# Four turned spectra instead of three, later products, and a last half chunk rebuilt by matmuls in the first convolution of an S4 and attention kernel

## The chip, the cores and the metric

The kernel runs on one core of a Trainium2 chip. The metric is the device time of one execution in microseconds (us). Before the change the median is 611.42 us over 3 runs (610.12 to 612.61). Engines are named as in the profile: PE is TensorE, PEld its weight loads, DVE is VectorE, ACT is ScalarE, POOL is GpSimd, SP is SyncE, which here issues the DMAs.

Times inside an execution ("229.3") are microseconds from the start of the profiled span.

## The reference, cut to what matters

```python
x = A_u                                                    # (1, 2048, 512), bf16
x = x + _A_ref(_layernorm(x), A_re, ..., log_dt, Dskip)    # the first conv: all of the change
x = x + _B_ref(_layernorm(x), wqkv, wo)                    # sliding local attention
x = x + _A_ref(_layernorm(x), ...)                         # same conv kernel again
x = x + _B_ref(_layernorm(x), wqkv, wo)

def _A_ref(u, ...):                                        # cut
    P = exp(dt * A * l)                                    # D=512 channels, N=128 states, L=2048 positions
    K = einsum("dn,dnl,dn->dl", Cc, P, dB).real            # the convolution kernel of each channel
    y = irfft(rfft(pad(u)) * rfft(pad(K)))[:L]             # FFT convolution over 2L
    return y + u * Dskip
```

Only the first conv builds `K`; the second reuses its spectra from DRAM.

## The kernel before

The first conv goes through eight half chunks of 64 channels, called stages 0 to 7 here (`hc` in the code). In each stage VectorE builds a table of powers (`seed`, `base`, then three `high` operations, then the `y_products` by `MPA` and `MPB`), and PE contracts the table to `K` (`contract`). Between them, chunk by chunk (128 channels), runs the FFT convolution. Its steps for a chunk are:

- a spectrum in two DFT factors: `first` (PE), copy to `Z` (ACT), `turn` (a transposing DMA of 256 KB into `zt`), `second` (PE), copy to `xc` or `Kt` (ACT);
- four products `pa`, `pb` of the signal's and the kernel's spectrum (DVE);
- four inverses (PE) and copies to `VT` (ACT), then `final` (PE) and copies to `X` (ACT).

The products of chunks 0, 1 and 2 come in stages 3, 5 and 7. Those of chunk 3 come in the tail, after the last table.

```python
class Conv:
    def __init__(...):
        self.xbar, self.ahead = True, 3
        self.w = tile_pool(name="f_w", bufs=self.ahead)     # slots of zt; KTq uses the same slots (tag "zt")

    def spectrum(self, rhs_j, n, dsts, drow=None):          # cut
        def turn(i):
            zt = self.w.tile([128, 4, 2, 128], BF, name="zt", tag="zt")
            nc.sync.dma_start(zt..., Z[:, i * 4:i * 4 + 4]..., transpose=True)
        def second(i):
            ...                                             # 4 matmuls from zt, copy by ScalarE to dsts[i]
            if i + self.ahead < cs:
                turn(i + self.ahead)                        # the fourth turn only after the first second
```

```python
# the order of stages 3 and 5: t are the table's steps (t[2] = high, t[3] = MPA, t[4] = MPB), ks the kernel's
# spectrum, p the products, v the inverses
play(t[:2], ks[5:6], [store], ks[6:7], p[:2], ks[7:9], p[2:3], v[:1], p[3:], v[1:3], t[2:3], v[3:], [fin],
     ks[9:], t[3:], [lambda: residual(dc)])

def contract(self, T, Y2, hc, half=None):                   # cut
    if half != 1:
        self.KTq = self.kq.tile([128, 1024], BF, name="KTq", tag="zt")
    nc.scalar.copy(KTq..., psk...)
    return lambda: nc.sync.dma_start(self.kscr[hc]..., KTq...)   # to DRAM, fetched back in another order

def spectrum32(self, KT, drow, dst, ps, Z):                 # half a chunk's spectrum, for the tail (cut)
    def first(jh):
        ...                                                 # half the positions at a time
        (nc.scalar.copy if jh == 0 else nc.vector.tensor_copy)(Z..., ps...)
    def turn():                                             # PE transposes
        ...
        (nc.vector.tensor_copy if r == 0 else nc.scalar.copy)(zt[:, r, :], pt[:, r]...)
    def second():
        ...
        (nc.scalar.copy if r == 0 else nc.vector.tensor_copy)(dst[:, r, :], xp[:])
```

Of the kernel before, what the change touches and what calls it, by code (L numbers as in the profile page):

```python
# [11 lines left out]
ALU = mybir.AluOpType  # L12
AX = mybir.AxisListType
F32 = mybir.dt.float32
BF = mybir.dt.bfloat16
# [4 lines left out]
D = 512  # L20
# [74 lines left out]
def make_consts(nc, const, C):  # L95
    fc = _fft_consts()
    bones_np = np.zeros((128, 4, 32), dtype=np.float32)
    for f in range(128):
        for k in range(4):
            bones_np[f, k, 8 * k + f // 16] = 1.0  # L100
    for name in ("F1", "F1T"):
        C[name + "_h"] = nc.inline_tensor(_bf(fc[name]), name="c_" + name)
    todo = [("ident", _bf(np.eye(128)), BF), ("C2", _bf(fc["C2"]), BF), ("IC", _bf(fc["IC"]), BF),
            ("onesr", _bf(np.ones((1, 128))), BF)]
    for name, arr, dt in todo:
        C[name] = load_const(nc, const, name, arr, dt)
    C["bones_np"] = _bf(bones_np)

# [30 lines left out]
class LnStats:  # L139


    def __init__(self, nc, pool, parts, nm, eps, tag=""):
        self.nc, self.parts, self.eps = nc, parts, eps
        self.st = pool.tile([128, NJ, len(parts), 6], F32, name="ln_st_" + nm, tag="ln_st" + tag)
        self.mv = pool.tile([128, NJ, 2], F32, name="ln_mv_" + nm, tag="ln_mv" + tag)
        self.den = pool.tile([128, NJ], BF, name="ln_den_" + nm, tag="ln_den" + tag)
        self.rstd = pool.tile([128, NJ], F32, name="ln_rstd_" + nm, tag="ln_rstd" + tag)
        self.nb = pool.tile([128, NJ], F32, name="ln_nb_" + nm, tag="ln_nb" + tag)
# [18 lines left out]
class Conv:  # L167


    def __init__(self, nc, tc, es, C, X, psA, psT, zbufs=2, pbufs=2, vbufs=1):  # L170
# [3 lines left out]
        self.xbar, self.ahead = True, 3  # L174
# [62 lines left out]
    def finish(self, dc, xc, Kt):  # L237

        nc, IC = self.nc, self.C["IC"]
        VT = self.one.tile([128, 2, NJ, DCH], BF, name="VT", tag="VT", bufs=self.vbufs)  # L240
        prod = {}

        def product(c):
            prod[c] = self.products(c, xc, Kt)

        def inverse(c):
            pa, pb = prod.pop(c)
            vp = self.pst([128, 2, 32, 2, 8])
            for g in range(4):
                sl = slice(g * 128, (g + 1) * 128)  # L250
                o = vp[:, g // 2, :, g % 2, :]
                nc.tensor.matmul(o, pa[:, 0, sl], IC[:, 0, :], start=True, stop=False)
                nc.tensor.matmul(o, pb[:, 1, sl], IC[:, 1, :], start=False, stop=False)
                nc.tensor.matmul(o, pb[:, 0, sl], IC[:, 2, :], start=False, stop=False)
                nc.tensor.matmul(o, pa[:, 1, sl], IC[:, 2, :], start=False, stop=True)  # L255
            self.vt_evac(c, vp, VT)

        return ([lambda c=c: product(c) for c in range(4)], [lambda c=c: inverse(c) for c in range(4)],
                lambda: self.final(dc, 0, DCH, VT, 8))

    def products(self, c, xc, Kt):
# [5 lines left out]
        return pa, pb  # L267

# [9 lines left out]

    def block(self, c, xc, Kt, VT):

        nc, IC = self.nc, self.C["IC"]
        y = self.w.tile([128, 2, 512], BF, name="y", tag="zt")

        def product():
            pa, pb = self.products(c, xc, Kt)
            nc.vector.tensor_tensor(y[:, 0, :], pa[:, 0, :], pb[:, 1, :], ALU.subtract)
            nc.vector.tensor_tensor(y[:, 1, :], pa[:, 1, :], pb[:, 0, :], ALU.add)

        def inverse():
            vp = self.pst([128, 2, 32, 2, 8])  # L290
            for g in range(4):
                sl = slice(g * 128, (g + 1) * 128)
                o = vp[:, g // 2, :, g % 2, :]
                nc.tensor.matmul(o, y[:, 0, sl], IC[:, 0, :], start=True, stop=False)
                nc.tensor.matmul(o, y[:, 1, sl], IC[:, 2, :], start=False, stop=True)
            self.vt_evac(c, vp, VT, (None, nc.vector if c == 3 else None))
        return [product, inverse]
# [20 lines left out]

    def spectrum32(self, KT, drow, dst, ps, Z):

# [3 lines left out]
        def first(jh):  # L324
            for j in range(jh * 8, jh * 8 + 8):
                for r in range(2):
                    o = ps[:, r, :, j * 8:(j + 1) * 8]
                    dk = j == 0 and r == 0
                    nc.tensor.matmul(o, F1[:, j, r, :], KT[:, :, j, :], start=True, stop=not dk)
                    if dk:  # L330
                        nc.tensor.matmul(o, self.C["onesr"][:], drow, start=False, stop=True)
            sl = slice(jh * 64, jh * 64 + 64)
            (nc.scalar.copy if jh == 0 else nc.vector.tensor_copy)(Z[:, :, :, sl].rearrange("p g r k -> p r g k"),
                                                                   ps[:, :, :, sl])

        def turn():
            pt = self.psT.tile([128, 2, 4, 128], BF, name="pt", tag="psT")
            zt = self.w.tile([128, 2, 512], BF, name="zt", tag="zt")
            for r in range(2):
                for g in range(4):  # L340
                    nc.tensor.transpose(pt[:, r, g, :], Z[:, g, r, :], ident[:])
                (nc.vector.tensor_copy if r == 0 else nc.scalar.copy)(zt[:, r, :],
                                                                      pt[:, r].rearrange("q g k -> q (g k)"))
            box.append(zt)

        def second():
            zt = box.pop()
            for r, (a, b) in ((0, (0, 2)), (1, (1, 0))):
                xp = self.psT.tile([128, 512], F32, name="xpu", tag="psT")
                nc.tensor.matmul(xp[:], C2[:, a, :], zt[:, 0, :], start=True, stop=False)  # L350
                nc.tensor.matmul(xp[:], C2[:, b, :], zt[:, 1, :], start=False, stop=True)
                (nc.scalar.copy if r == 0 else nc.vector.tensor_copy)(dst[:, r, :], xp[:])
        return [lambda: first(0), lambda: first(1), turn, second]
# [16 lines left out]
class Multipliers:  # L370


    def __init__(self, pool):
        self.one = pool.tile([128, 8, 2, HD, 2], BF, name="MU1")
# [227 lines left out]
def kernel_and_first_conv(nc, tc, C, prm, x2d, const, kt_dram, kscr, ln, eps):  # L602
    with ExitStack() as es:
        mt = es.enter_context(tc.tile_pool(name="k_mt", bufs=1))
        M = Multipliers(mt)
        cb = mt.tile([128, 8, HD, 2, 2], BF, name="cb")
        psk = es.enter_context(tc.tile_pool(name="k_psk", bufs=1, space=PSUM))
        T = Tables(nc, tc, es, M, cb, psk, kscr)
        with tc.tile_pool(name="k_prep", bufs=1) as pp, tc.tile_pool(name="k_pst", bufs=2, space=PSUM) as pst:
            raw = load_params(nc, pp, prm)  # L610
# [16 lines left out]
        ln_b = LnStats(nc, const, [(0, 3 * DCH), (3 * DCH, D - 64), (D - 64, D)], "b", eps)  # L627
# [51 lines left out]
        def k_fft(KT, dc, h0=0, h1=2):  # L679
            n = (h1 - h0) * 64  # L680
            drow = skip_row(dc)[:, h0 * 64:h0 * 64 + n]
# [11 lines left out]
        VTs, fetches = [], []  # L693

        def tail(store, ks, p, v, fin, t):
            play(t[:2], ks[5:6], [store])
            KT = k_fetch(3, 0, 1)
            play(ks[6:7], p[:2], ks[7:9], p[2:3], v[:1], p[3:], v[1:2])
            k3 = k_fft(KT, 3, 0, 1)
            Kt, xc = Kts[3], xcs.pop(3)  # L700
            Drow = skip_row(3)
            play(k3[:4], ks[9:], k3[4:5], v[2:3], t[2:3], v[3:], [fin], t[3:4])
            store = contract(7, 0)
            play(k3[5:7], [store, lambda: residual(3)])
            KT = kp.tile([128, 2, 4, NJ, 8], BF, name="KTu", tag="KT")

            def fetch(u):
                return nc.sync.dma_start(KT[:, u].rearrange("p g j d -> p g (j d)"),
                                         kscr[7][:, :, u * 128:u * 128 + 128].rearrange("g p x -> p g x"))
            fetch(0)  # L710
            play(t[4:])
            store = contract(7, 1)
            store()
            fetches.append(fetch(1))
            VT = cv.one.tile([128, 2, NJ, DCH], BF, name="VT", tag="VT", bufs=1)
            VTs.append(VT)
            for c in range(2):
                play(cv.block(c, xc, Kt, VT))
            Z = cv.z.tile([128, 16, 2, 128], BF, name="Z", tag="Z")
            u = [cv.spectrum32(KT[:, n], Drow[:, 64 + n * 32:96 + n * 32], Kt[:, 2 + n],  # L720
                               psk.tile([128, 2, 4, 128], F32, name="psu", tag="psk") if n == 0 else
                               cv.pst([128, 2, 4, 128]), Z[:, n * 4:n * 4 + 4]) for n in range(2)]
            ln_b.gather(X, 0, 0, 6)
            play(u[0][:2])
            cv.final(3, 0, 64, VT, 8)
            ln_b.gather(X, 0, 6, 9)
            play(u[0][2:3])
            ln_b.gather(X, 0, 9, NJ)
            play(u[0][3:4], u[1][:2])
            b = cv.block(2, xc, Kt, VT)  # L730
            play(b[:1], u[1][2:3], b[1:], u[1][3:])
            ln_b.gather(X, 1, 0, NJ)
            play(cv.block(3, xc, Kt, VT))

        with tc.manual_schedule():
            us = u_fft(0)
            play(tables(0), us[:5])
            for hc in range(1, 8):
# [11 lines left out]
                else:  # L750
                    store = contract(hc - 1)
                    p, v, fin = cv.finish(dc - 1, xcs.pop(dc - 1), Kts.pop(dc - 1))
                    if hc == 7:
                        break
                    play(t[:2], ks[5:6], [store], ks[6:7], p[:2], ks[7:9], p[2:3], v[:1], p[3:], v[1:3], t[2:3], v[3:], [fin],
                         ks[9:], t[3:], [lambda: residual(dc)])
            tail(store, ks, p, v, fin, t)
        nc.sync.dma_start(kt_dram[3], Kts[3][:])
        VT = VTs[0]
# [6 lines left out]
        cv.final(3, 64, 128, VT, 4, after)  # L766
# [318 lines left out]
def kernel(  # L1085
# [25 lines left out]
    ln = LnStats(nc, const, [(0, D)], "a", eps)  # L1111
    X, ln_b, marks, last_fetch = kernel_and_first_conv(nc, tc, C, prm, A_u[0], const, kt_dram, kscr, ln, eps)
# [41 lines left out]
```

## Time and profile before

The first conv takes 36 to 264 us of the 607. VectorE is its busiest engine. The page's first part, kernel before (busy us, share of the span, instructions):

```profile
span 607.3 us, 13074 instructions
PE 429.0 (71%) x5646; PEld 285.4 (47%) x5674; DVE 497.4 (82%) x835; ACT 323.5 (53%) x458; POOL 12.6 (2%) x50
```

Busy time in windows, kernel before. The columns are the window, its length, then the busy us and instructions of each engine, the granted TensorE clock, the DMA share and GB/s:

```profile
36.00:62.00 26.00, 2.98 (x16) 1.68 (x16) 25.41 (x43) 26.00 (x43) 0.00 (x0) 1.00 0.00 0
62.00:99.00 37.00, 22.12 (x605) 14.26 (x605) 36.17 (x39) 17.59 (x20) 0.47 (x4) 0.90 0.56 101
229.30:261.10 31.80, 17.60 (x290) 11.56 (x291) 21.46 (x55) 10.91 (x18) 6.06 (x1) 0.75 0.44 135
```

In the first two windows VectorE is busy nearly throughout (25.41 of 26, 36.17 of 37; in the first ScalarE is full as well). From 99 us on, only its waits before the products interrupt it, as the next view shows, so there a saved VectorE wait is saved time. In the third, the tail, nothing is full: VectorE 21.5 of 31.8, PE 17.6, ACT 10.9. That is a chain of hops between engines.

Where VectorE stands still before the tail, its timeline shows. These are the `pa` products of stage 3 (start, busy us, operation, and in brackets the idle time before it and what ended it; the lines between them are left out):

```profile
109.59 0.69 DVE L265 TENSOR_TENSOR pa<-xc,Kt 128x1024 bf16<-128x1024 bf16 x1 [1.71 <-ACT Kt L221]
112.35 0.69 DVE L265 TENSOR_TENSOR pa<-xc,Kt 128x1024 bf16<-128x1024 bf16 x1 [1.47 <-ACT Kt L221]
118.93 0.69 DVE L265 TENSOR_TENSOR pa<-xc,Kt 128x1024 bf16<-128x1024 bf16 x1 [5.29 <-issue]
120.68 0.69 DVE L265 TENSOR_TENSOR pa<-xc,Kt 128x1024 bf16<-128x1024 bf16 x1 [0.45 <-issue]
```

The four brackets add up to 8.9 us. The same sums are 6.5 us in stage 5 and 5.2 us in stage 7: 20.6 us in all. The view of waits, VectorE from 99 to 222 us (total us, times, longest):

```profile
DVE pa L265 <- ACT Kt L221: 14.0, 6, 3.6
DVE pa L265 <- issue: 6.6, 4, 5.3
```

These are the only waits of VectorE in that stretch. SyncE's timeline says why `Kt` is late. In stage 3 the first three turns are issued at 103.03, 105.24 and 106.64, but the fourth only at 111.30, when a slot of `zt` is free; it lands at 114.34. By the order of the code the slot that the first `second` gives back (it ends at 107.59) goes to `KTq`, whose copy starts at 107.63. The fourth turn gets the slot of the next `second`, which ends at 111.27. PE kept to the order of the code meanwhile: the first pair of products ends at 110.89 and both accumulator tiles are copied out by 113.24, but the inverse starts only at 115.30, behind the four matmuls of the fourth `second` (from 114.39), for whose turn PE stood idle 2.25 us.

### The profile page before, as it was taken

The page shows a single profiled execution, that of the slowest core. Times are in us where ns is not written, and L with a number is a line of the kernel's source. Part 1 is how long each engine was busy: PE and PEld are TensorE (multiplying, and loading weights), DVE is VectorE, ACT ScalarE, POOL GpSimd, SP SyncE. Part 2 cuts the span into 40 slices and gives each one's busy share as a digit, 9 for nine tenths or more (in the row PEclk, how much of TensorE's full clock was granted, in tenths as well). Part 3 has the DMA queues.
Part 4 walks back from the last instruction along what each step waited for, and adds up shares of the span by engine and source line. Part 5 has one row for each costly group of instructions (what it writes and reads, how often), then busy time and mean ns, then how long its engine had stood idle before and what let it go on. Part 6 is the DMA issues. An engine that isn't in the chain of part 4 may idle for free.

```text
span 607.3 us, 13074 instructions
## 1 busy us (share of the span) xinstructions
PE 429.0 (71%) x5646; PEld 285.4 (47%) x5674; DVE 497.4 (82%) x835; ACT 323.5 (53%) x458; POOL 12.6 (2%) x50
## 2 busy tenths in 40 slices
PE   1101575665685687479987779978995899858996
PEld 0101343453362465254365566656764434727763
DVE  5999999499699877765977899859999588689950
ACT  4999644454463555236584223467973556722144
POOL 0000000000000003000000000000000000000000
PEclk9999978898897698659998699989998799968999
DMA  9100464635546545400004060000000000040011
GB/s 287 68 1 0 69 108 89 146 50 103 90 105 124 88 123 128 156 0 1 2 2 115 6 257 23 1 1 1 1 2 1 2 0 2 1 121 1 2 70 70
DMA packets 56031, 36.62 MB, mean 60 GB/s; under 512 B 46762, under 2 KB 51754, under 8 KB 54694
## 3 DMA queue, kind: packets, MB, share of 16 engines
q1 hardware_dynamic: 54390, 35.40, 23.2%
q8 instruction: 44, 0.72, 0.5%
q10 hardware_dynamic: 1584, 0.39, 0.3%
q14 instruction: 13, 0.11, 0.1%
HBM read 15.90 MB, written 8.39 MB: 40 GB/s over the span
## 4 chain that ended last, share of the span: by engine, by line
PE 25%; DVE 22%; ACT 7%; issue 6%; POOL 0%; POOLq 0%; ACTq 0%
PE ps_qk L930 8%; DVE prod L1032 6%; PE ps_o L1056 4%; PE ps_v L942 4%; DVE ln_st_b L153 2%; PE Lp L976 2%; PE pt_x L910 2%; PE po L1047 2%; DVE pa L827 2%; DVE pb L828 1%; DVE prod L971 1%; DVE VT L850 1%; DVE zt L809 1%; PE ps_o L1058 1%; ACT oT L1050 1%
## 5 line engine op out<-in xcount | busy, mean ns | idle before, releaser
L1047 PE MATMUL po<-sb_ident,prod 128*128 128x128 bf16 x1024 | 71.5, 230 | 12.6 <-DVE prod L1032 9.1
L1047 PEld LDWEIGHTS <-prod 128*128 128x128 bf16 x1024 | 63.6, 103 | 22.1 <-DVE prod L1032 18.8
L930 PE MATMUL ps_qk<-xnT,wqk 128*128 128x512 bf16 x245 | 64.2, 393 | 4.4 <-ACT xnT L915 2.3
L963 DVE TENSOR_TENSOR prod<-qT,kT 128x2048 bf16<-128x2048 bf16 (+3 forms) x48 | 43.2, 952 | 14.2 <-ACT qT L932 7.2
L195 PEld LDWEIGHTS <-sb_F 128*128 128x128 bf16 x256 | 21.6, 123 | 58.0 <-issue 56.8
L1032 DVE TENSOR_TENSOR prod<-V,L 128x2048 bf16<-128x2048 bf16 (+3 forms) x48 | 43.6, 947 | 6.4 <-PE po L1047 6.4
L1050 ACT CAST oT<-po 128x1024 bf16<-128x1024 f32 x16 | 15.4, 1015 | 56.6 <-PE po L1047 56.6
L195 PE MATMUL psA<-X,sb_F 128*128 128x128 bf16 x128 | 13.3, 255 | 42.4 <-ACT X L624 33.2
L971 DVE TENSOR_TENSOR prod<-qT,kT 128x2048 bf16<-128x2048 bf16 (+3 forms) x40 | 34.9, 902 | 6.9 <-ACT kT L932 4.3
L930 PEld LDWEIGHTS <-wqk 128*128 128x128 bf16 x256 | 23.6, 101 | 32.5 <-issue 12.4
L1056 PE MATMUL ps_o<-wo_t,oT 128*128 128x512 bf16 x121 | 33.5, 380 | 4.7 <-ACT oT L1050 3.9
L1032 DVE TENSOR_TENSOR prod<-Vp,L 128x2048 bf16<-128x2048 bf16 (+3 forms) x40 | 34.9, 896 | 0.0
L198 ACT CAST Z<-psA 128x1024 bf16<-128x1024 f32 (+1 forms) x32 | 29.0, 966 | 9.7 <-PE psA L195 9.7
L976 PE MATMUL Lp<-prod,sb_bones 128*32 128x512 bf16 x256 | 25.4, 416 | 9.6 <-DVE prod L971 4.9
L584 PE MATMUL psk<-Ttab 128*32 128x64 bf16 x1024 | 22.2, 204 | 13.3 <-issue 13.3
L217 PE MATMUL psA<-zt,sb_C 128*128 128x512 bf16 x30 | 12.9, 430 | 25.4 <-DMA zt<-Z 24.7
L942 PE MATMUL ps_v<-wv,xnT 128*128 128x256 bf16 x256 | 28.6, 273 | 1.7 <-ACT V L945 1.7
L594 ACT CAST KTq<-psk 128x1024 bf16<-128x1024 f32 (+1 forms) x9 | 8.3, 918 | 39.5 <-PE psA L220 38.8
L265 DVE TENSOR_TENSOR pa<-xc,Kt 128x1024 bf16<-128x1024 bf16 x16 | 11.0, 690 | 22.0 <-ACT Kt L221 15.4
L566 DVE TENSOR_TENSOR Ttab<-Ttab,MPA 128x2048 bf16<-128x2048 bf16 (+2 forms) x20 | 27.7, 1432 | 0.0
L275 ACT CAST VT<-psA 128x512 bf16<-128x512 f32 x31 | 16.7, 589 | 20.5 <-PE psA L255 9.9
L942 PEld LDWEIGHTS <-xnT 128*128 128x128 bf16 x256 | 25.0, 98 | 5.3 <-issue 2.1
(193 smaller groups left out, 1084.4 us busy)
## 6 DMA issues: line engine op xcount, KB each, us to landing
X<-in_A_u_dram SPq DMA_DIRECT2D x8, 512.0 KB, 5.3
kt_scratch<-Kt SPq DMA_DIRECT2D x4, 1024.0 KB
Kt<-kt_scratch SPq DMA_DIRECT2D x4, 1024.0 KB, 7.9
Vp<-V SPq DMA_DIRECT2D x2, 1568.0 KB
out_dram<-X SPq DMA_DIRECT2D x4, 512.0 KB, 2.6
k_scratch<-KTq SPq DMA_DIRECT2D x7, 256.0 KB, 2.3
KT<-k_scratch SPq DMA_DIRECT2D x7, 256.0 KB, 2.8
sb_F<-c_F SPq DMA_DIRECT2D x1, 1024.0 KB, 7.3
```

The source lines that it names most:

```text
L195: nc.tensor.matmul(o, F1[:, j, r, :], rhs_j(j), start=True, stop=not dk)
L198: nc.scalar.copy(Z[:, 0:n // 8, :, jq * 32:(jq + 1) * 32].rearrange("p g r k -> p r g k"), ps[:, :, 0:n // 8, :])
L566: nc.vector.tensor_tensor(dst, src.to_broadcast([128, q, n, 2 * EYB]), mm.to_broadcast([128, q * n, EYB, 2]), ALU.mult)
L584: nc.tensor.matmul(o.rearrange("e (s i) -> e s i", s=2), xs, T[:, 1:3, h, m // 2, :, t], start=(m == 0), stop=False, skip_group_check=True)
L930: nc.tensor.matmul(ps[:], wqk[:, ct, f0:f0 + 128], xnT[:, ct, s0:s0 + 512], start=(ct == 0), stop=(ct == 3))
L942: nc.tensor.matmul(ps[:, jj].rearrange("p t h d -> p (t h d)"), xnT[:, ct, (j + jj) * 128:(j + jj + 1) * 128], wv[:, ct, a * 256:(a + 1) * ...
L963: nc.vector.tensor_tensor(pr[:, :, (ja - j0) * 128:(ja - j0) * 128 + n], qT[fp][:, :, ja * 128: ja * 128 + n], kT[fp][:, :, (ja - sh) * 12 ...
L971: nc.vector.tensor_tensor(pr[:, :, 0:n], qT[fp][:, :, q0: q0 + n], kT[fp][:, :, k0: k0 + n], ALU.mult)
L976: nc.tensor.matmul(Lp[r0:r0 + 32, w // 4, :], bones[:, w % 4, :], pr[:, f2, hb * 512:(hb + 1) * 512], start=(w % 4 == 0), stop=(w % 4 == 3 ...
L1032: nc.vector.tensor_tensor(p2[:, ja - j0: ja - j0 + n, :].rearrange("p j (t d h) -> p (j t) d h", t=2, d=DH), src.rearrange("p j (t d h) -> ...
L1047: nc.tensor.matmul(po[f2][:, jj, :], p2[:, jj, f2 * 128:(f2 + 1) * 128], ident[:], start=(w == 0 and jj % 4 == 0), stop=(w == W - 1), skip ...
L1056: nc.tensor.matmul(ps[:], oT[:, ft, j * 128:(j + 1) * 128], wo_t[:, ft, :], start=(ft == 0), stop=False)
```

## The change

Its intent:

1. Four turned spectra in flight (`ahead` 3 to 4). To find the room, the layernorm statistics move to other memory.
2. In stages 3 and 5 the `high` operations are issued ahead of the first product and the `MPA` operations between the second and third, so that VectorE has work while it would wait. In stage 7 `high` moves likewise.
3. A new tail. The last half chunk's `K` no longer goes to DRAM and back to be reordered; matmuls with a 0/1 matrix (`spread`) move its rows. The copies of the tail move from VectorE to ScalarE, and statistics fill VectorE meanwhile.

```diff
-        self.xbar, self.ahead = True, 3
+        self.xbar, self.ahead = True, 4
```
```diff
-                    play(t[:2], ks[5:6], [store], ks[6:7], p[:2], ks[7:9], p[2:3], v[:1], p[3:], v[1:3], t[2:3], v[3:], [fin],
-                         ks[9:], t[3:], [lambda: residual(dc)])
+                    play(t[:2], ks[5:6], [store], ks[6:9], t[2:3], p[:2], v[:1], t[3:4], p[2:3], v[1:2], p[3:], v[2:], [fin],
+                         ks[9:], t[4:], [lambda: residual(dc)])
```
```diff
+    spread = np.zeros((128, 4, 132), dtype=np.float32)
+    for p in range(128):
+        spread[p, p // 32, 4 * (p % 32) + 3] = 1.0
...
+            def spread_rows(n):
+                kq = T.KTq[:, n * 512:n * 512 + 512].rearrange("p (c x) -> p c x", c=4)
+                pk = psT.tile([128, 4, NJ, 8], F32, name="pk", tag="psT")
+                for g in range(4):
+                    for c in range(4):
+                        nc.tensor.matmul(pk[:, g].rearrange("p j d -> p (j d)"), spread[:, g, 3 - c:131 - c],
+                                         kq[:, c], start=(g == 0 and c == 0), stop=(c == 3), skip_group_check=True)
+                nc.scalar.copy(KTu[:, n].rearrange("p j g d -> p g j d"), pk[:])
...
-            (nc.scalar.copy if jh == 0 else nc.vector.tensor_copy)(Z[:, :, :, sl].rearrange("p g r k -> p r g k"),
-                                                                   ps[:, :, :, sl])
+            nc.scalar.copy(Z[:].rearrange("p g r k -> p r g k"), ps[:])
...
+            spread_rows(0)
+            contract(7, 1)
+            play(u[0][:1])
+            spread_rows(1)
+            ln_b.gather(X, 0, 0, NJ)
...
+            play(u[0][2:3], k3[5:6], u[1][:1], u[0][3:4], k3[6:7], u[1][2:3], b[:1], [fin], b[2:3], binv[:1], u[1][3:], b[1:2],
+                 binv[2:3], b[3:], binv[1:2], binv[3:])
...
-        cv.final(3, 64, 128, VT, 4, after)
+        cv.final(3, 0, 128, VT, 4, after)
```

## The prediction

> **What bounds it now.** Only the first conv (36 to 264 us of 607) changes. VectorE (DVE) bounds it: the busy-time windows give it 25.4 of 26 us at 36-62, 32.2 of 33 at 62-95, 31.2 of 33 at 167-200. Its idle time is before the `pa` products (DVE timeline): stage 3 1.71 + 1.47 + 5.29 + 0.45 = 8.9 us, stage 5 6.5, stage 7 5.2; the view of waits puts 15.4 us on `Kt` (ACT) and 6.6 on issue, where the two product buffers wait for the inverse. Then the last table ends at 229.3 and the last `VT` copy at 261.1: 31.8 us with DVE busy 21.5, PE 17.6: a chain of hops.
>
> **Mechanism.** The fourth turn (DMA transpose) waits for a free slot: in stage 3 it is issued at 111.30, the third at 106.64, and lands at 114.34. The four seconds precede the inverse in PE's queue, so the inverse waits, then the products. Turns issued together are spaced about 1.3 us, so the fourth should land some 3 us earlier. One is 256 KB; [...] bursts of about 210 GB/s, 1.25 us.
>
> **Stages 3, 5, 7.** The instruction order puts the three `high` operations (3.67 us) ahead of the first product, and in stages 3 and 5 the `MPA` operations (3.4 us) between the second and third. No DVE work is removed. The store of `KTq` no longer queues behind the fourth turn (142.59 in stage 4), so the next `KT` fetch comes about 3 us earlier.
> - Stage 3: all 8.9 us hidden.
> - Stage 5: DVE arrives 9 us earlier, PE's chain only 5 to 6; 2 to 3 us of wait remain: gain 4.
> - Stage 7: likewise, and only `high` moved: gain 2.
>
> Together 15 us at the end of the last table.
>
> **Tail.** Removed: store and fetch of both halves of the last half chunk (2.5 + 5.1 us per trip), and 4.3 us of DVE copies (Z, zt, Kt, VT), now on ACT. Added: 32 selection matmuls [...] and two 0.6 us ACT copies. The 16 statistics (estimated 0.34 us each from the 384- and 64-column ones: 5.4 us) fill DVE while PE rebuilds. Estimated last table to last `VT` copy: 24 to 29 us against 31.8, gain 3 to 8. Later layers only start earlier. The weight load waits for the second selection, still before its use.
>
> **Prediction.** 611.4 - 20 = 591 us, 8 in 10 within 584 to 598. Faster by over 2%: 0.90; within: 0.09; slower: 0.01.
>
> **Right or wrong in the profile.** Four turns at 1.3 us spacing; stage 3 products without `Kt` waits; DVE waits on `pa` down from 22 to 6-9 us; last table operation ending near 214; first `xn` (264.4 before) near 243-245; no `k_scratch` traffic for chunk 7; later stages unchanged in length.
>
> **What would make it wrong.** PE becoming the bound of stages 5 and 7: PE plus its DMA waits is an estimated 40 us per two stages, against 42 of DVE work; more throttling (granted 0.85 there) would bring the waits back. In the tail everything is on ACT and an in-order PE with two accumulator tiles; at the clock of 0.58 seen at 245-265 the chain could be as long as before.

The sum was 15 us at the end of the last table and 3 to 8 us in the tail, together taken as 20: 611.4 - 20 = 591 us. The estimated 40 us of PE can be read from the trace: in the 48.9 us of stages 4 and 5 (132.0 to 180.9) PE was busy for 30.7 us and waited 11.0 us for DMAs, 41.7 us in all, and VectorE was busy for 41.6 us. The "in-order PE" is what stage 3 above shows (the inverse at 115.30 behind the fourth `second` at 114.39). That a clock below the 0.85 of 167 to 200 us would bring the waits back was a guess, which no run tests.

## More of the kernel before

VectorE in the tail (cut to the chain of the first 32 channels):

```profile
234.85 2.85 DVE L153 BATCH_NORM_STATS2 ln_st_b<-X 128x6 f32<-128x384 bf16 x6
239.19 0.69 DVE L333 CAST Z<-psu 128x512 bf16<-128x512 f32 x1 [1.50 <-ACT Z L333]
239.80 1.47 DVE L153 BATCH_NORM_STATS2 ln_st_b<-X 128x6 f32<-128x384 bf16 x3
241.91 0.42 DVE L342 COPY zt<-pt 128x512 bf16<-128x512 bf16 x1 [0.63 <-PE pt L341]
242.25 3.31 DVE L153 BATCH_NORM_STATS2 ln_st_b<-X 128x6 f32<-128x384 bf16 x7
245.47 0.68 DVE L352 CAST Kt<-xpu 128x512 bf16<-128x512 f32 x1
```

The copies of the chain (`Z`, `zt`, `Kt`) stand in VectorE's queue between the layernorm statistics of the next layer. ACT wrote the other half of `zt` by 243.40, but this half of `Kt` follows only at 245.47, behind seven statistics.

## The result and the profile after

The changed kernel takes 588.36 us (median of 4 runs, 585.19 to 590.48) beside 611.27 us (610.12 to 612.61). The ratio is 0.962, with a 95% interval of 0.957 to 0.967. A ratio here is the mean time of one kernel's fast runs over that of the other's of the same rounds, so it is not quite the ratio of the medians.

The page's first part, kernel after, then its windows with the new tail as the third:

```profile
span 586.6 us, 13076 instructions
PE 429.5 (73%) x5670; PEld 281.0 (48%) x5670; DVE 492.5 (84%) x828; ACT 326.5 (56%) x459; POOL 12.6 (2%) x50
```

```profile
36.00:62.00 26.00, 2.98 (x16) 1.67 (x16) 25.41 (x44) 26.00 (x43) 0.00 (x0) 1.00 0.00 0
62.00:99.00 37.00, 22.78 (x617) 14.27 (x617) 36.18 (x39) 19.28 (x21) 0.47 (x4) 0.89 0.56 101
217.10:236.60 19.50, 16.60 (x316) 11.71 (x314) 15.46 (x44) 15.99 (x23) 6.06 (x1) 1.00 0.57 188
```

Up to 99 us VectorE's busy time is the same. The tail is 19.5 us long instead of 31.8, and PE and ACT are now busy in over four fifths of it.

VectorE in stage 3, kernel after (the end of `high`, the `pa` products and `MPA`; the lines between them are left out):

```profile
110.27 1.23 DVE L548 TENSOR_TENSOR Ttab<-Ttab,tx 128x2048 bf16<-128x2048 bf16 x1
111.41 0.68 DVE L270 TENSOR_TENSOR pa<-xc,Kt 128x1024 bf16<-128x1024 bf16 x1
112.61 0.69 DVE L270 TENSOR_TENSOR pa<-xc,Kt 128x1024 bf16<-128x1024 bf16 x1
113.82 3.42 DVE L566 TENSOR_TENSOR Ttab<-Ttab,MPA 128x2048 bf16<-128x2048 bf16 x2
117.16 0.68 DVE L270 TENSOR_TENSOR pa<-xc,Kt 128x1024 bf16<-128x1024 bf16 x1
118.36 0.68 DVE L270 TENSOR_TENSOR pa<-xc,Kt 128x1024 bf16<-128x1024 bf16 x1
```

No bracket is left: `high` and `MPA` stand where the waits were. The four turns are issued at 101.20, 103.36, 104.66 and 106.24, and the fourth lands at 110.28. The view of waits, VectorE from 99 to 222 us, kernel after:

```profile
DVE pa L270 <- ACT Kt L226: 6.2, 3, 2.7
DVE pa L270 <- issue: 2.9, 2, 2.4
```

The 20.6 us are now 9.0 us: none in stage 3, 2.7 us in stage 5, 6.3 us in stage 7.

VectorE in the new tail, kernel after (cut to the statistics and the products before which it waits):

```profile
216.97 5.32 DVE L158 BATCH_NORM_STATS2 ln_st_b<-X 128x6 f32<-128x256 bf16 x16
223.94 0.69 DVE L270 TENSOR_TENSOR pa<-xc,Kt 128x1024 bf16<-128x1024 bf16 x1 [1.65 <-ACT Kt L226]
...
230.36 0.69 DVE L270 TENSOR_TENSOR pa<-xc,Kt 128x1024 bf16<-128x1024 bf16 x1 [2.21 <-ACT X L316]
```

The copies of the chain are on ScalarE now, and the statistics run while VectorE has nothing else to do.

The gain of 20.7 us of span falls into four stretches, read from the traces (the last table operation is the last `Y2tab` product; the last `VT` copy ends the tail; the first attention product is the first `prod<-qT,kT`):

| stretch | before | after | gain |
|---|---|---|---|
| start to end of the last table operation | 229.3 | 217.1 | 12.2 |
| to the end of the last `VT` copy (tail) | 31.8 | 19.5 | 12.3 |
| to the first attention product | 19.6 | 22.6 | -3.0 |
| to the end | 326.6 | 327.5 | -0.9 |

Two gains of 12 us stand against a loss of 3 us at the entry of the attention. The experiments ask which part of the change made each.

### The profile page after: what moved, and what is told of

It is laid out like the page before. It is cut to its first block, busy times and chain, and to the rows that moved or that the text cites. A ratio compares the mean times of both kernels' runs of the same rounds, so it can differ in the third digit from the quotient of the medians.

```text
span 586.6 us, 13076 instructions
## 1 busy us (share of the span) xinstructions
PE 429.5 (73%) x5670; PEld 281.0 (48%) x5670; DVE 492.5 (84%) x828; ACT 326.5 (56%) x459; POOL 12.6 (2%) x50
## 4 chain that ended last, share of the span: by engine, by line
PE 35%; DVE 25%; ACT 20%; issue 9%; DMA 8%; SPq 1%; POOL 0%; ACTq 0%; POOLq 0%; DVEq 0%
PE ps_qk L933 8%; DVE prod L1035 6%; DMA zt<-Z 4%; PE ps_o L1059 4%; PE ps_v L945 4%; ACT Z L203 3%; PE Lp L979 2%; ACT X L625 2%; PE po L1050 2%; PE pt_x L913 2%; DVE ln_st_b L158 2%; PE psA L200 2%; DVE pa L830 2%; DVE pb L831 2%; DVE prod L974 2%
## 5 line engine op out<-in xcount | busy, mean ns | idle before, releaser
L1050 PE MATMUL po<-sb_ident,prod 128*128 128x128 bf16 x1024 | 71.8, 230 | 12.2 <-DVE prod L1035 8.7
L933 PE MATMUL ps_qk<-xnT,wqk 128*128 128x512 bf16 x256 | 65.9, 395 | 4.9 <-ACT xnT L918 2.3
L200 PEld LDWEIGHTS <-sb_F 128*128 128x128 bf16 x256 | 18.9, 112 | 59.4 <-issue 58.6
L200 PE MATMUL psA<-X,sb_F 128*128 128x128 bf16 x128 | 12.2, 238 | 43.4 <-ACT X L625 33.3
L974 DVE TENSOR_TENSOR prod<-qT,kT 128x2048 bf16<-128x2048 bf16 (+3 forms) x40 | 34.9, 900 | 6.9 <-ACT kT L935 4.3
L566 DVE TENSOR_TENSOR Y2tab<-Ttab,MPB 128x6144 bf16<-128x6144 bf16 (+1 forms) x13 | 27.2, 2118 | 0.0
L1062 ACT CAST X<-ps_o 128x512 bf16<-128x512 f32 x32 | 18.2, 586 | 15.2 <-PE ps_o L1061 15.2
L935 ACT CAST kT<-ps_qk 128x512 bf16<-128x512 f32 x32 | 18.8, 590 | 12.5 <-PE ps_qk L933 12.3
```

Of the source, the lines that this page charges most:

```text
L200: nc.tensor.matmul(o, F1[:, j, r, :], rhs_j(j), start=True, stop=not dk)
L566: nc.vector.tensor_tensor(dst, src.to_broadcast([128, q, n, 2 * EYB]), mm.to_broadcast([128, q * n, EYB, 2]), ALU.mult)
L933: nc.tensor.matmul(ps[:], wqk[:, ct, f0:f0 + 128], xnT[:, ct, s0:s0 + 512], start=(ct == 0), stop=(ct == 3))
L974: nc.vector.tensor_tensor(pr[:, :, 0:n], qT[fp][:, :, q0: q0 + n], kT[fp][:, :, k0: k0 + n], ALU.mult)
L1050: nc.tensor.matmul(po[f2][:, jj, :], p2[:, jj, f2 * 128:(f2 + 1) * 128], ident[:], start=(w == 0 and jj % 4 == 0), stop=(w == W - 1), skip ...
```

## The experiments

Names beginning with `b_` start from the kernel before, those with `a_` from the changed kernel. All twelve runs gave correct results and were timed in 5 rounds beside the kernel before, whose medians were 612.1, 612.8, 611.87 and 612.83 us in the four sets. In the table "waits" are VectorE's idle times before the four `pa` products of stages 3, 5 and 7, from one profile each.

| run | median us (range) | ratio to before, 95% | waits in stages 3 / 5 / 7, sum | last table ends | tail | tail to attention product |
|---|---|---|---|---|---|---|
| before | 611.27 (610.12 to 612.61) | | 8.9 / 6.5 / 5.2, 20.6 | 229.3 | 31.8 | 19.6 |
| after | 588.36 (585.19 to 590.48) | 0.962 (0.957 to 0.967) | 0 / 2.7 / 6.3, 9.0 | 217.1 | 19.5 | 22.6 |
| b_turns | 599.32 (596.35 to 603.10) | 0.981 (0.976 to 0.985) | 2.6 / 2.7 / 2.9, 8.2 | 216.9 | 31.7 | 20.0 |
| b_order | 611.53 (609.46 to 616.12) | 1.000 (0.996 to 1.005) | 2.8 / 5.6 / 12.7, 21.1 | 229.5 | 33.6 | 20.2 |
| b_turns_order | 603.79 (602.24 to 605.04) | 0.987 (0.983 to 0.990) | 0 / 4.2 / 10.0, 14.2 | 222.3 | 32.7 | 20.7 |
| a_three | 600.43 (597.08 to 603.93) | 0.981 (0.977 to 0.986) | 4.3 / 8.7 / 8.8, 21.7 | 230.2 | 19.4 | 22.8 |
| a_oldorder | 588.49 (587.48 to 590.44) | 0.961 (0.958 to 0.965) | 5.2 / 3.4 / 1.2, 9.8 | 218.5 | 20.0 | 22.8 |
| a_mix | 584.62 (581.97 to 589.45) | 0.956 (0.951 to 0.960) | 0.5 / 3.9 / 1.3, 5.8 | 214.0 | 19.3 | 23.8 |
| a_mix_again | 586.41 (582.22 to 587.25) | 0.954 (0.951 to 0.957) | 2.2 / 4.1 / 1.2, 7.6 | 215.6 | 19.8 | 23.8 |
| a_trip | 595.84 (593.70 to 597.27) | 0.973 (0.969 to 0.976) | 0 / 3.9 / 5.9, 9.9 | 218.1 | 26.2 | 22.6 |
| a_dvecopies | 599.83 (598.10 to 601.33) | 0.980 (0.976 to 0.983) | 0 / 3.9 / 6.0, 9.9 | 218.1 | 28.9 | 24.8 |
| a_dvec_late | 595.48 (594.52 to 597.90) | 0.972 (0.968 to 0.976) | 0 / 3.8 / 5.7, 9.5 | 217.5 | 23.8 | 26.9 |
| a_trip_dvec | 606.18 (603.98 to 609.62) | 0.990 (0.986 to 0.994) | 0 / 2.4 / 4.4, 6.8 | 215.0 | 34.9 | 26.4 |
| a_best | 589.24 (586.77 to 592.98) | 0.962 (0.957 to 0.966) | 4.0 / 3.6 / 2.1, 9.7 | 217.9 | 19.7 | 23.3 |

One relation holds in all fourteen rows: the end of the last table minus the sum of the waits is 208.0 to 208.7 us. VectorE bounds the part up to the last table, its work there is fixed, and its waits before the products are the only thing that moves that end.

A single profile carries chance of its own. The kernels after, a_trip, a_dvecopies, a_dvec_late and a_trip_dvec give VectorE the same work in the same order up to the last table, and end it at 215.0 to 218.1. Differences of 3 us at this mark are therefore not evidence; 12 us are. The profile of b_turns is that of its fastest execution (596.35 us beside its median of 599.32), so the medians are given beside the marks.

### Which part made the 12 us up to the last table

**b_turns: the kernel before with four turns only**, and the statistics moved to make room.

```diff
-        self.xbar, self.ahead = True, 3
+        self.xbar, self.ahead = True, 4
...
+            ln = LnStats(nc, pp, [(0, D)], "a", eps)
...
+            ln_b = LnStats(nc, const, [(0, 3 * DCH), ...], "b", eps, st=(T.wk, "tb"))
```

> The kernel before with four turned spectra in flight and nothing else of the change (the statistics tiles move to find the room). Marks read from the trace: last table operation ends at 229.3 in the kernel before and 217.0 in the changed one; first xn 264.4 and 240.6. Theory (turns and order each hide a part): the fourth spectrum lands about 3 us earlier in stages 3, 5 and 7, the KT fetch comes some 3 us earlier, waits before the pa products fall from 20.6 to about 15 us, last table operation near 224, time 605 to 607. Rival A (the order of the products is all of it): time within 1 us of 611, last table operation 228 to 229. Rival B (the turns are all of it): last table operation 217 to 219, time near 600.

**b_order: the kernel before with only the later products in stages 3 and 5** (three turns stay).

```diff
-                    play(t[:2], ks[5:6], [store], ks[6:7], p[:2], ks[7:9], p[2:3], v[:1], ... t[2:3], v[3:], [fin], ...
+                    play(t[:2], ks[5:6], [store], ks[6:9], t[2:3], p[:2], v[:1], t[3:4], p[2:3], v[1:2], p[3:], ...
```

> The kernel before with the products of stages 3 and 5 issued one table stage later, three spectra in flight. Theory: stage 3 hides its Kt waits and part of the wait for the inverse (gain about 6), but stage 5 then waits for a PE and DMA chain that is not shorter (gain about 1): last table operation 221 to 223, time 603 to 606. Rival A (the order is all of it): last table operation 217 to 219, time near 600. Rival B (turns are all): 611.

**b_turns_order: both edits**, with the old order of stage 7 and the old tail.

> Both of them with the old tail (its DRAM trip, its order and stage 7 as before). Theory: the stage part of the gain is there without the new tail: last table operation 217 to 219 (10 to 12 us), then the old tail of about 32 us to the last VT copy and 35 to xn: time 599 to 601. If the new tail lengthened or shortened the stages, this mark differs from 217 by more than 2.

**a_three: the changed kernel with three turns.**

```diff
-        self.xbar, self.ahead = True, 4
+        self.xbar, self.ahead = True, 3
```

> The changed kernel with three turned spectra in flight again. Theory: it gives back what the fourth is worth beside the new order, 3 to 6 us: last table operation 220 to 223, time 592 to 594. Rival A (the order is all of it): 588 to 589, last table operation 217. Rival B (turns are all): last table operation 227 to 229, time near 599.

Measured: b_turns ends the last table at 216.9, as the changed kernel does (217.1), and its tail is the old one (31.7 us). Its median is 12.8 us below that of the kernel before in the same rounds (599.32 and 612.1). VectorE at the `pa` products of stage 3 in b_turns:

```profile
107.83 0.69 DVE L266 TENSOR_TENSOR pa<-xc,Kt 128x1024 bf16<-128x1024 bf16 x1
109.57 0.69 DVE L266 TENSOR_TENSOR pa<-xc,Kt 128x1024 bf16<-128x1024 bf16 x1 [0.46 <-ACT Kt L222]
112.56 0.69 DVE L266 TENSOR_TENSOR pa<-xc,Kt 128x1024 bf16<-128x1024 bf16 x1 [1.69 <-ACT Kt L222]
114.31 0.69 DVE L266 TENSOR_TENSOR pa<-xc,Kt 128x1024 bf16<-128x1024 bf16 x1 [0.45 <-issue]
```

The same four products as in the kernel before, in the old order, wait 2.6 us instead of 8.9. a_three loses the whole stage gain again (230.2) and keeps the whole gain of the tail (19.4). b_order gains nothing. Waits of VectorE from 99 to 222 us in b_order:

```profile
DVE pa L265 <- ACT Kt L221: 19.5, 6, 7.3
DVE pa L265 <- issue: 1.6, 4, 0.5
```

The order took 6.1 us out of stage 3 and 0.9 out of stage 5, and gave 7.5 back in stage 7. So the theory, in which turns and order each hide a part, fell. The fourth turn alone is worth the 12 us; the order of stages 3 and 5 only moved waits.

b_turns_order missed its expectation (217 to 219 and 599 to 601 us): its last table ends at 222.3 and it takes 603.79 us. Beside four turns and with the old stage 7, the new order thus cost 5.4 us at the mark and 4.5 us in the median (599.32 for b_turns in the same rounds). The changed kernel, with the new stage 7 and the new tail, ends at 217.1. Moving `high` ahead in stage 7 may give the 5 us back, but no run changes stage 7 alone.

The edit of `ahead` does two things in one: it adds a slot, and it issues all four turns before `KTq` takes one. A slot of its own for `KTq` would also have let the fourth turn go earlier; that was not tested.

**a_oldorder: the changed kernel with the old order in stages 3 and 5.** This asks the same from the other side.

```diff
-                    play(t[:2], ks[5:6], [store], ks[6:9], t[2:3], p[:2], v[:1], t[3:4], p[2:3], v[1:2], p[3:], v[2:], [fin],
-                         ks[9:], t[4:], [lambda: residual(dc)])
+                    play(t[:2], ks[5:6], [store], ks[6:7], p[:2], ks[7:9], p[2:3], v[:1], p[3:], v[1:3], t[2:3], v[3:], [fin],
+                         ks[9:], t[3:], [lambda: residual(dc)])
```

> The changed kernel with stages 3 and 5 in the old order (the MPA operations after the second product, the three high operations after the fourth); four turned spectra, the new order of stage 7 and the new tail stay. Theory formed from the first batch (the fourth turn alone gives the whole stage gain; the order only moves the wait from stage 3 to stages 5 and 7): last table operation ends at 214 to 217 us as against 217.05, time within 1% of the changed kernel, most likely 586 to 589 us. Rival (the order is needed beside the fourth turn): last table operation at 220 us or later, time 592 us or more.

Measured: 588.49 us against the changed kernel's 588.36. The last table ends at 218.5, which is 1.5 us outside my range and inside the spread named above. The time is what the theory said: with four turns and the new stage 7, the reordering of stages 3 and 5 is worth nothing.

**a_mix: the three `high` operations singly between the products in stages 3 and 5**, and `MPA` back behind them (`high(0)` to `high(2)` stand for the three, shortened here).

```diff
-                    play(t[:2], ks[5:6], [store], ks[6:9], t[2:3], p[:2], v[:1], t[3:4], p[2:3], v[1:2], p[3:], v[2:], [fin],
-                         ks[9:], t[4:], [lambda: residual(dc)])
+                    play(t[:2], ks[5:6], [store], ks[6:9], p[:2], [high(0)], v[:1], p[2:3],
+                         [high(1)], v[1:2], p[3:], [high(2)], v[2:], [fin],
+                         ks[9:], t[3:], [lambda: residual(dc)])
```

> The changed kernel with the three high operations of stages 3 and 5 spread singly between the products (product 0, product 1, high 0, product 2, high 1, product 3, high 2) and MPA back after the products. Theory: what limits is the loop through PE from the third product over the inverse, the next Kt and back, 38 to 41 us per two stages, so filling VectorE at the second and third gaps without delaying the first product cuts the pa waits by about 1 us a stage: last table operation at 213 to 216 us, time 584 to 588 us. Rival (VectorE order does not matter at all once four turns are in flight): last table operation within 0.7 us of that of the run with the old order.

The 38 to 41 us of the theory were my estimate. PE's busy time and its waits for DMAs are 30.7 + 11.0 = 41.7 us over stages 4 and 5 of the kernel before and 31.0 + 5.8 = 36.8 us in the changed kernel (122.8 to 167.7); that the loop limits is not shown.

Measured: 584.62 us, with the last table ending at 214.0 and waits of 5.8 us. Both are as the theory expected. But the mark alone doesn't show that filling the gaps helped: a_trip_dvec, in the order of the changed kernel, ends its last table at 215.0. The last run returns to this.

### Which part made the 12 us of the tail

**a_trip: the changed kernel with the DRAM trip back**, all else of the new tail kept.

```diff
-                for g in range(4):
-                    for c in range(4):
-                        nc.tensor.matmul(pk[:, g]..., spread[:, g, 3 - c:131 - c], kq[:, c], ...)
-                nc.scalar.copy(KTu[:, n].rearrange("p j g d -> p g j d"), pk[:])
+                nc.sync.dma_start(KTu[:, n]..., kscr[7][:, :, n * 128:n * 128 + 128]...)
...
-            contract(7, 0)
+            contract(7, 0)()          # and the store of the other half likewise
```

> The changed kernel with the last half chunk rebuilt by the DRAM trip (store of KTq, fetch of the reordered block) in place of the selection matmuls and their two copies; everything else of the new tail stays. Theory: the trip lay on the chain; it costs 2.5 + 5.1 us where selection matmuls and copy cost about 2.2 us, so last table to last VT copy becomes 24 to 26 us as against 19.5, time 593 to 595 us. Rival (the trip was hidden, the gain of the tail comes from the copies moved to ScalarE and the new order): 19.5 to 20.5 us, time as the changed kernel.

Measured: the tail takes 26.2 us instead of 19.5, and the time is 595.84 us. Both are slightly above my ranges; the theory holds and the rival doesn't. The waits in a_trip's tail (218 to 249 us):

```profile
DVE pa L270 <- ACT Kt L226: 8.1, 1, 8.1
ACT Z L335 <- PE psA L332: 6.1, 1, 6.1
...
PE psA L332 <- DMA KTu<-k_scratch: 5.5, 1, 5.5
```

Read from the bottom, PE waits 5.5 us for the fetch, ACT for PE, VectorE for ACT. Store and first fetch landed 2.47 and 4.05 us after their issue. In the changed kernel 16 selection matmuls take 1.06 us and the copy behind them 0.60 us.

**a_dvecopies: the changed kernel with half of the tail's copies on VectorE**, split as in the kernel before.

```diff
-            nc.scalar.copy(Z[:].rearrange("p g r k -> p r g k"), ps[:])
+            for h in range(2):
+                sl = slice(h * 64, h * 64 + 64)
+                (nc.scalar.copy if h == 0 else nc.vector.tensor_copy)(Z[:, :, :, sl]..., ps[:, :, :, sl])
...             # zt (r = 0), Kt (r = 1) and half of the last VT likewise
```

> The changed kernel with half of the tail's copies back on VectorE as before (half of Z, r0 of zt, r1 of Kt, half of the last VT), selection matmuls stay. Theory: these copies wait in VectorE's queue behind statistics and products, so last table to last VT copy grows by 1 to 3 us, to 20.5 to 22.5 us. Rival A (the copies are most of the tail's gain): over 24 us. Rival B (halving each copy over two engines shortens the chain more than the queue delays it): 19.5 us or less.

Measured: 28.9 us of tail. My theory (1 to 3 us more) fell and rival A held: these copies cost 9.4 us. VectorE's timeline from 220 us in a_dvecopies shows how:

```profile
221.57 0.69 DVE L337 CAST Z<-psA 128x512 bf16<-128x512 f32 x1 [3.48 <-ACT Z L337]
222.18 5.31 DVE L158 BATCH_NORM_STATS2 ln_st_b<-X 128x6 f32<-128x256 bf16 x16
227.41 0.41 DVE L347 COPY zt<-pt 128x512 bf16<-128x512 bf16 x1
```

The copy to `zt`, 0.41 us long, stands behind 16 statistics. VectorE took them in the order of issue: 5.31 us of work that nobody waits for delays 0.41 us that everybody waits for. ScalarE, which writes the other half of `zt`, stood idle for 5.45 us before it, until this copy.

**a_dvec_late: a_dvecopies with those statistics at the end of the tail**, a bad place for speed, on purpose.

```diff
-            ln_b.gather(X, 0, 0, NJ)
             VT = cv.one.tile(...)
...
+            ln_b.gather(X, 0, 0, NJ)
             ln_b.gather(X, 1, 0, NJ)
```

> The run with half of the tail's copies on VectorE, but with the 16 statistics of the first 256 columns (5.3 us) moved from between the first and second of these copies to the end of the tail, behind the last product. Wrong place for speed, on purpose: it separates the copies' own time from their place in VectorE's in-order queue. Theory (the 9.4 us that the copies on VectorE cost came from waiting behind the statistics): last table to last VT copy falls from 28.9 to 20 to 23 us; the statistics then delay the end, so the time stays within 5 us of that run's 599.8. Rival (copies on VectorE are slow in this chain wherever the statistics are): 26 us or more.

Measured: the tail takes 23.8 us, 0.8 us above my range and well below the rival's 26. VectorE's timeline in a_dvec_late:

```profile
221.69 0.69 DVE L337 CAST Z<-psA 128x512 bf16<-128x512 f32 x1 [4.15 <-ACT Z L337]
223.45 0.42 DVE L347 COPY zt<-pt 128x512 bf16<-128x512 bf16 x1 [1.07 <-PE pt L345]
```

The copy to `zt` starts 1.76 us after that to `Z`, instead of 5.84 us (227.41 and 221.57 in a_dvecopies). So of the 9.4 us, 5.1 went with the statistics ahead of the copy. The other 4.3 us were not taken apart: the copies and hops are in them, and a lower TensorE clock (0.93 instead of 1.00 in the tail). The statistics at the end then make the stretch to the attention 26.9 us, as designed.

**a_trip_dvec: both undone**, the trip and the copies on VectorE (the two edits above together).

> The changed kernel with both undone: the DRAM trip in place of selection matmuls and half of the tail's copies on VectorE. One alone cost 6.7 us (trip: 26.2 us from last table to last VT copy) and 9.4 us (copies: 28.9 us) over 19.5 us. Theory (the copies cost so much because 5.3 us of statistics stand ahead of them; with the trip, the statistics pass while the fetch is under way): the costs don't add; last table to last VT copy 28 to 31 us, time 599 to 603 us. Rival (they add): 35 us or more, time 605 us or more.

Measured: the tail takes 34.9 us and the time is 606.18 us; the rival asked for 35 and 605 or more. My theory said that the statistics would pass while the fetch is under way. That was wrong: the costs nearly add (19.5 + 6.7 + 9.4 = 35.6). VectorE's timeline in a_trip_dvec:

```profile
224.88 0.69 DVE L337 CAST Z<-psA 128x512 bf16<-128x512 f32 x1 [9.91 <-ACT Z L337]
225.49 5.32 DVE L158 BATCH_NORM_STATS2 ln_st_b<-X 128x6 f32<-128x256 bf16 x16
230.72 0.41 DVE L347 COPY zt<-pt 128x512 bf16<-128x512 bf16 x1
```

The same queue explains it. The copy to `Z` stands ahead of the statistics and itself waits for the fetch, 9.91 us. The statistics did not start in that hole; they started behind it (225.49) and again held up `zt`. I had thought of what stands ahead of `zt` and not of what stands ahead of the statistics.

The old tail (31.7 to 33.6 us in the four kernels that have it) is even shorter than this one, probably since its statistics were cut into pieces of 6, 3 and 7 and its order fitted its copies; no run tests that. Thus the parts of the new tail are not independent improvements: taking out either the selection matmuls or the ScalarE copies loses half or more of the 12.3 us, and what is left of the new tail without both is about 3 us slower than the old one.

The granted clock moves along with these tails and was not separated from them. What a lower one does to the matmuls shows in stage 3 of the kernel before: the matmuls of the inverse (128x256) start 0.21 us apart at a granted clock of 0.50 (115.3 to 118.4) and 0.11 us apart at 1.00 (118.7 to 120.3). The clock was 1.00 in the changed kernel's tail, 0.80 in a_trip, 0.88 in a_dvecopies, 0.93 in a_dvec_late, 0.75 in a_trip_dvec and 0.75 before. PE's busy time in the tail was 16.7 us in the changed kernel and, for the same matmuls, 19.3 in a_dvecopies and 17.6 in a_dvec_late. So up to 2.6 of the 9.4 us, and up to 1.6 of the 5.1, may be slower matmuls.

### A faster version?

**a_best: a_mix with two more edits.** In the tail, `final` of chunk 2 comes behind the first inverse; in the first attention layer all copies of `xnT` are on VectorE.

```diff
-            play(..., b[:1], [fin], b[2:3], binv[:1], u[1][3:], b[1:2],
+            play(..., b[:1], b[2:3], binv[:1], u[1][3:], [fin], b[1:2],
...
-                if j2 % 2 == 0:
+                if j2 % 2 == 0 or store is None:
                     nc.vector.tensor_copy(dst, pt[:])
```

> The run with high operations between the products (584.6 us, last table operation at 214.0, last table to last VT copy 19.3, first xn to first attention product 19.8), with two more changes: in the tail the final of chunk 2 is issued behind the first inverse and the second spectrum's second instead of ahead of them, and the copies of xnT in the first attention layer are all on VectorE. Theory: the first inverse then frees its product buffer before the two X copies, the 2.2 us wait of the second pair of products goes and ScalarE, which bounds the tail, still has all its copies: last table to last VT copy 18.0 to 18.6; at the attention's entry ScalarE's queue no longer holds kT behind xnT: first xn to first product 17.5 to 19 us. Time 581 to 584 us. Rival (ScalarE's work alone sets the tail, the scheduler's order the entry): both distances within 0.4 us of before.

Measured: 589.24 us. The tail (19.7 against 19.3) did not get shorter, and the first `xn` to the first product took 19.3 against 19.8 us, hardly more than the 0.4 us that the rival allowed. Neither edit paid; the stretch to the attention is not mended by this. But the last table ended at 217.9, 3.9 us later than in a_mix, though no instruction up to there had changed its place.

**a_mix_again: a_mix unchanged, once more**, on another chip.

> The run with high operations between the products, unchanged, once more. The run made from it with two more edits came out 4.6 us slower (589.2 against 584.6), although every engine has the same instructions in the same order up to the last table operation and its profile was already 3.9 us behind there (217.9 against 214.0), in stage 3, where its granted clock was 0.81 against 0.92. Theory A (the difference is between chips or executions, through the granted clock in stage 3; spreading the high operations is worth little or nothing): 586 to 590 us, ratio to before 0.958 to 0.964, and the mark of the last table operation follows the clock of stage 3. Theory B (spreading is worth about 1 per cent and the two edits cost 4 us): 582 to 586 us, ratio 0.951 to 0.958, last table operation at 213.5 to 215 us.

Measured: 586.41 us, ratio 0.954 (0.951 to 0.957), last table at 215.6. The median is at the edge that both theories shared, the ratio speaks for B, and the mark lies above B's range (213.5 to 215). The clock does not sort the profiles as theory A wanted. Windows of a_mix (first fence), a_mix_again (second) and a_best (third) around stage 3:

```profile
99.40:109.00 9.60, 5.88 (x265) 4.06 (x265) 9.26 (x16) 3.03 (x4) 0.24 (x2) 0.81 1.03 140
109.00:122.00 13.00, 11.47 (x113) 9.21 (x112) 12.49 (x13) 7.55 (x12) 0.00 (x0) 1.00 0.49 122
```

```profile
99.40:109.00 9.60, 5.15 (x263) 3.25 (x263) 9.26 (x15) 3.06 (x4) 0.24 (x2) 0.98 0.96 133
109.00:122.00 13.00, 11.66 (x95) 8.48 (x93) 10.77 (x13) 6.83 (x12) 0.00 (x0) 0.88 0.50 127
```

```profile
99.40:109.00 9.60, 6.37 (x274) 4.43 (x271) 8.28 (x14) 3.18 (x4) 0.24 (x2) 0.68 0.71 72
109.00:122.00 13.00, 11.54 (x76) 7.72 (x77) 9.97 (x13) 7.96 (x13) 0.00 (x0) 0.87 0.68 172
```

The third number from the end is the granted clock. a_best had the lowest in the first window (0.68, and its DMA share was behind as well, 0.71), and it waited longest in stage 3. But a_mix with 0.81 was ahead of a_mix_again with 0.98. These three profiles of the same stage show that the granted clock varies from execution to execution, between 0.68 and 0.98 in the first window; that the clock causes the spread of the mark, they do not.

What stands: over twelve runs on two chips a_mix took 581.97 to 589.45 us, mean 585.3, where a_oldorder's six had a mean of 588.7 and the changed kernel's four 588.1. It beats the kernel before by over 4% and is probably half a per cent faster than the changed kernel; that half per cent was never timed side by side. Why a_best came out 4 us behind it stays open between its two edits and the executions.

## Why the prediction was right or wrong

The total was right: 591 us, with 584 to 598 as the range, against 588.36. That hit is in part luck: the stages gave 2.8 us less than forecast and the later layers lost 3.9 us, which cancelled nearly all of what the tail gave beyond its range's middle (12.3 us against 3 to 8), and one mechanism was credited wrongly.

- **"All 8.9 us hidden" in stage 3.** The number was right: the waits went from 8.9 to 0 and stage 4 begins 9.2 us earlier (132.0 to 122.8). The cause was not. I credited the order of the instructions; b_turns shows that the fourth turn alone removes 6.3 us of the 8.9 and what is left does not cost later stages, while b_order shows that order alone hides as much of stage 3 and pays it all back by stage 7.
- **"Stage 5 ... gain 4."** Measured 4.0 us: stage 6 begins 13.2 us earlier (180.9 to 167.7), 9.2 of them already gained.
- **"Stage 7 ... gain 2."** This step failed: the waits of stage 7 rose from 5.2 to 6.3 us, so it lost about 1 us. Together "15 us at the end of the last table" measured 12.2. The prediction named the reason among its risks ("PE becoming the bound of stages 5 and 7"): the products delayed in stages 3 and 5 delay the inverses and the next spectrum on PE, and the wait reappears as a late `Kt`. That this path through PE is the cause was argued from the order of the queues; that delayed products in stages 3 and 5 make stage 7 wait, b_turns against b_turns_order shows (2.9 against 10.0 us), and a_oldorder against the changed kernel (1.2 against 6.3).
- **"Gain 3 to 8" in the tail.** This term was mis-sized: it measured 12.3. I counted the trip mostly as hidden, but undoing it costs 6.7 us. I counted the 4.3 us of VectorE copies by their length, but undoing their move costs 9.4 us, 5.1 of which go when the statistics ahead of the copies go. The selection matmuls took 0.066 us each (16 in 1.06). I feared a low clock; the new tail, denser on PE (busy for 16.6 of 19.5 us instead of 17.6 of 31.8), was granted 1.00 instead of 0.75. Why, is not shown: no run separates the clock from the rest here.
- **"Later layers only start earlier."** This was wrong by 3.9 us. The stretch from the last `VT` copy to the first attention product grew from 19.6 to 22.6 us, and the rest by 0.9. All kernels with the old tail show 19.6 to 20.7 us here, all with the new one at least 22.6. In the new tail the last `final` covers 128 columns instead of 64 (each copy to `X` 0.58 to 0.59 us instead of 0.37), and VectorE is busy for 14.2 us of this stretch instead of 12.4. The clock is not the cause: it was higher (0.92 against 0.72). Taking all copies of `xnT` off ScalarE won 0.5 us at most (a_best). The cause is not settled.
- **"DVE waits on `pa` down from 22 to 6-9."** With the tail's products counted, as in the 22.0 of the page, 12.9 us are left: 9.0 up to the last table and 3.9 in the tail, where the predicted range left room for none. The last table ended at 217.1 instead of "near 214", and the first `xn` came at 240.6 instead of 243 to 245, since the tail gained more than forecast.
- **The turns.** "Spaced about 1.3 us" held in part: the gaps in stage 3 are 2.16, 1.30 and 1.58 us. Over the 30 turns of the kernel before, one occupies SP's queue for 1.23 to 2.38 us, median 1.31. 256 KB in 1.25 us are about 210 GB/s, and while three turns follow each other (issued from 66.19 to 70.31) the trace shows mostly 180 to 225 GB/s once the first is moving. In the kernel before the fourth turn, issued apart from the others, landed 3.04 us after its issue. In stage 3 it was late because it waited for its slot (issued at 111.30, the third at 106.64), and then took this time to land.

## What to carry to other kernels

When the same wait repeats stage after stage and its release is a late transfer, count the slots first: one more buffer took out 12.4 of 20.6 us, while reordering work into the gaps on the waiting engine moved them to a later stage. Here b_turns and a_three agree on it from both sides (waits of 8.2 us with four turns in the kernel before, 21.7 us with three in the changed one). In a chain that hops between engines, an operation cost here what stood ahead of it in its engine's queue (5.31 us of statistics ahead of a copy of 0.41 us in a_dvecopies): look at what the filler work waits behind as well as at what waits behind the filler (some 4 of the 9.4 us here), and take short links of the chain off the engine that does the long fillers.

## Figures that these traces give

- A transposing DMA of 256 KB issued apart from the others landed after 3.04 us (kernel before, 111.30 to 114.34), and in stage 3 each occupied the issuing queue for 1.23 to 2.17 us. Over the 30 of the kernel before, issue to landing took 3.0 to 5.0 us, median 3.5.
- For a store followed by a fetch of the same 128 KB in another order, here through SP's queue with other transfers under way, the traces show 2.49 + 5.15 us in the old tail (7.6 us) and 2.47 + 4.05 us in a_trip (6.5 us).
- The layernorm statistics operation on VectorE took 0.33 us for 256 columns (16 in 5.32 us), 0.20 us for 128 (16 in 3.19 us), 0.47 us for 384 (7 in 3.31 us), bf16 in.
- Five kernels with the same VectorE work up to the mark ended the last table 3.1 us apart (215.0 to 218.1), which is half a per cent of the whole time, so here changes under 1% need several runs side by side. That the clock causes this spread is not shown.
